# One more visit turns its attention weights on VectorE and DMAs, two visits become a pair, and six steps round two pieces of weights where three did

## The chip, the cores and the metric

The kernel runs on one core of one Trainium2 chip. The metric is device time in microseconds (us) of one execution. The kernel before takes 1389.05 us (median of three). TensorE is PE in the profile, its weight loads PEld, VectorE is DVE, ScalarE is ACT, GpSimd is POOL, SyncE is SP.

## The reference

Threshold attention over 8 batches of 8 heads, 576 positions, head size 64, followed by an MLP with a squared ReLU (condensed here):

```python
scores = scale * np.matmul(q, k.transpose(0, 1, 3, 2))
thresh = np.max(scores, axis=-1, keepdims=True) - tau
scores = np.where(scores >= thresh, scores, -1000000000.0)
attn = np.exp(scores - np.max(scores, axis=-1, keepdims=True))
attn = attn / (np.sum(attn, axis=-1, keepdims=True) + 1e-09)
out = np.matmul(attn, v)                 # (B,H,S,D) -> (B*S, H*D) = (4608, 512)
h = out @ w_in                           # 512 x 2048
r = np.maximum(h, 0.0)
y = (r * r) @ w_out                      # 2048 x 512
```

## The kernel before

Two things run through each other: attention, in *visits* (one pair of heads each) of four or five *steps* (128 query rows each), and the MLP in chunks of 256 tokens, cut into pieces of about 1.76 us of TensorE work that fill the steps.

The attention weights of a step must be transposed before they meet the values. Early visits do it on TensorE (`turn`), later ones on VectorE in blocks of 32x32 (`turn_blocks`), and DMAs then put the blocks in place (`place_blocks`). In the paired form two visits share one step for their last 64 rows each.

```python
def paired(n):
    return n >= 3 * HP            # HP = 4: visit 12 on
def by_dma(n):
    return n >= 3 * HP - 1        # visit 11 goes by DMA, alone
```

Each step stands in the program in this order. The scores need the two score banks of the step before (`s0`, `s1`, one buffer each), so they wait for that step's thresholding:

```python
            if now:
                round_weights(now[0], 0)         # ScalarE prepares the first piece
            if s != 1:
                scores(s)                        # TensorE, then VectorE's maximum
        # ... cut: turn(*old, 0), turn(*old, 1)
        if on:
            exponents(n, i)                      # ScalarE
            for p in now[1:]:
                round_weights(p, 0)              # ScalarE prepares a second piece
            # ... cut
            if lay:
                prep(n + 1)
            elif now:
                for p in now:
                    round_weights(p, 1)          # VectorE: a shift
        # ... cut: mix, fill
        if on:
            threshold(n, i)                      # VectorE: frees the score banks
            # ... cut
            if now:
                round_weights(now[0], 2)         # VectorE: a mask
                round_weights(now[0], 3)         # GpSimd
            for p in now[1:]:
                round_weights(p, 2)
                round_weights(p, 3)
```

`now` holds the pieces of MLP weights that are rounded in this step, none, one or two. There are 32, and their scratch space is the buffer that the turned blocks use later, so that the roundings must be done before the first visit that goes by DMA:

```python
        if s < HP * FIRST:                       # the first eight steps
            x = int(n > 0 and i == 0)
        else:
            x = 2 if (n, i) in ((2 * HP - 2, FIRST + 1), (2 * HP - 1, FIRST + 1), (2 * HP, FIRST)) else 1
        # ... cut
    assert out_from <= first_dma
```

After that, 16 subtractions on VectorE (`some_sums`) make the sums of weights that save an eighth of the later products. Each piece of the first half of MLP chunk 1 brings one along.

## Time and profile before

| kernel before | |
|---|---|
| time, median of 3 | 1389.05 us |
| profiled execution, span | 1389.8 us |
| TensorE busy / idle | 1354.5 / 35.3 us |
| TensorE idle in steps 8 to 29 (53.5 to 191.3 us) | 11.2 us |
| TensorE idle in steps 30 to 44 (to 310.0 us) | 2.7 us |

A step begins here at its first maximum on VectorE. The idle time is the step's length less TensorE's busy time in it. What the table tells is that the kernel is bound by TensorE nearly everywhere, and that what isn't lies in the start and in the steps with roundings. (The 35.3 us also hold 13.7 us before step 8 and 7.6 us after step 44.)

### The profile page before, as it was taken

Reading aid. Unit: us, or ns where it says so; the run is one execution under the profiler, and the core shown is the slowest. Engines: PE = TensorE matmul, PEld = TensorE weight load, DVE = VectorE, ACT = ScalarE, POOL = GpSimd, SP = SyncE. Lnnn points to the kernel's source line nnn. Section 1 sums busy time; section 2 is a strip of 40 time slices with the busy share of each in tenths; the row PEclk is TensorE's granted clock in tenths of the full one; section 3 lists DMA queues with packets and bytes.
Section 4 is the critical chain, followed back from the end, with each engine's and each line's share of the span. In section 5 each row is a group of like instructions: output and inputs, shape, how many; then the busy total and the mean of one; then the engine's idle time right before and its main releaser. Section 6 shows DMA issues by size and latency. Waiting matters only on the chain.

```text
span 1389.8 us, 22678 instructions
## 1 busy us (share of the span) xinstructions
PE 1354.5 (97%) x7576; PEld 1039.6 (75%) x7576; DVE 828.9 (60%) x1866; ACT 439.8 (32%) x1068; POOL 899.3 (65%) x1211
## 2 busy tenths in 40 slices
PE   6898999999999999999999999999999999999998
PEld 5676556777777777787777778777777877788887
DVE  5877675967767676757565757566666665401001
ACT  4776674223232323232223232322222222210110
POOL 3678875668786968686767677676867655422332
PEclk8999999999999999999999999999999999999999
DMA  8763531445545455554445355544445544310000
GB/s 154 157 152 107 143 93 29 88 85 106 115 98 115 97 109 114 105 112 94 92 87 113 76 111 107 112 87 97 93 93 91 118 89 102 64 31 16 0 16 16
DMA packets 407748, 127.95 MB, mean 92 GB/s; under 512 B 390832, under 2 KB 396752, under 8 KB 407632
## 3 DMA queue, kind: packets, MB, share of 16 engines
q1 hardware_dynamic: 385344, 94.57, 36.1%
q0 software_dynamic: 19984, 31.63, 8.4%
q8 instruction: 61, 1.00, 0.3%
q10 hardware_dynamic: 2304, 0.29, 0.2%
q14 instruction: 55, 0.45, 0.1%
HBM read 50.59 MB, written 9.44 MB: 43 GB/s over the span
## 4 chain that ended last, share of the span: by engine, by line
PE 89%; DVE 3%; ACT 3%; POOL 2%; issue 1%; DMA 1%; SPq 0%; DVEq 0%; ACTq 0%; POOLq 0%
PE bank L480 34%; PE bank L552 29%; PE s L246 12%; PE bank L432 11%; PE bank L519 2%; PE bank L330 2%; ACT wT L331 1%; ACT w L284 1%; DVE wo L507 1%; DVE w L296 1%; DVE st L268 1%; POOL g L491 0%; POOL w L306 0%; POOL w_in_sb L147 0%; DVE wo L296 0%
## 5 line engine op out<-in xcount | busy, mean ns | idle before, releaser
L480 PE MATMUL bank<-xT,w_in_sb 128*128 128x256 f32 x2304 | 520.4, 382 | 3.2 <-POOL w_in_sb L147 2.1
L480 PEld LDWEIGHTS bank<-xT,w_in_sb 128*128 128x128 f32 x2304 | 430.8, 190 | 85.8 <-issue 22.2
L268 DVE TENSOR_REDUCE st<-s 128x1 f32<-128x576 f32 x286 | 204.1, 753 | 224.4 <-PE s L246 224.3
L296 DVE SCALAR_TENSOR_TENSOR w<-s,st,w 128x576 f32<-128x576 f32 x269 | 209.2, 815 | 120.6 <-ACT w L284 120.5
L552 PE MATMUL bank<-wo,gsum 128*128 128x256 f32 x1088 | 248.9, 382 | 2.4 <-POOL gsum L470 2.4
L306 POOL TENSOR_SCALAR w<-w,st 128x576 f32<-128x576 f32 x269 | 223.5, 840 | 25.2 <-DVE st L299 19.2
L552 PEld LDWEIGHTS bank<-wo,gsum 128*128 128x128 f32 x1088 | 203.9, 190 | 41.5 <-issue 9.8
L491 POOL TENSOR_TENSOR g<-g 128x512 f32<-128x512 f32 x144 | 152.1, 1057 | 96.4 <-ACT g L490 95.1
L281 ACT ACTIVATE st<-st 128x2 f32<-128x2 f32 (+1 forms) x148 | 30.3, 205 | 566.1 <-DVE st L268 565.4
L552 PE MATMUL bank<-wo,g 128*128 128x256 f32 x816 | 188.3, 382 | 0.0
L284 ACT ACTIVATE w<-s,st 128x576 f32<-128x576 f32 x269 | 183.3, 732 | 0.2 <-ACT st L282 0.2
L370 DVE STREAM_TRANSPOSE turned<-w 128x512 f32<-128x512 f32 (+2 forms) x388 | 168.8, 490 | 18.7 <-DMA wT<-turned 16.7
L246 PE MATMUL s<-kT,qT 64*128 64x288 f32 x1016 | 166.9, 435 | 12.1 <-DVE kT L226 4.9
L304 POOL TENSOR_SCALAR st<-st 128x2 f32<-128x2 f32 (+1 forms) x148 | 32.9, 222 | 221.6 <-DVE w L296 214.4
L552 PEld LDWEIGHTS bank<-wo,g 128*128 128x128 f32 x816 | 153.0, 190 | 30.0 <-issue 8.7
L432 PE MATMUL bank<-wT,vs 128*64 128x128 f32 (+7 forms) x1700 | 167.8, 356 | 5.1 <-ACT wT L331 3.5
L432 PEld LDWEIGHTS bank<-wT,vs 128*64 128x64 f32 (+1 forms) x1700 | 95.5, 136 | 76.8 <-issue 24.6
L490 ACT ACTIVATE g<-bank 128x512 f32<-128x512 f32 x144 | 86.1, 599 | 194.8 <-PE bank L480 194.2
L246 PEld LDWEIGHTS s<-kT,qT 64*128 64x128 f32 x1016 | 94.9, 189 | 69.1 <-issue 49.0
L190 POOL DMA_DIRECT2D vs<-in_v_dram x144 | 90.7, 635 | 0.0
L566 DVE TENSOR_TENSOR gsum<-g 128x512 f32<-128x512 f32 x34 | 23.0, 707 | 110.6 <-PE bank L552 110.6
L145 POOL TENSOR_TENSOR turned<-turned 128x512 f32<-128x512 f32 x32 | 41.1, 1288 | 40.7 <-DVE turned L143 34.9
(80 smaller groups left out, 1006.1 us busy)
## 6 DMA issues: line engine op xcount, KB each, us to landing
wT<-turned SPq DMA_DIRECT2D x800, 72.0 KB, 2.3
out_dram<-osb POOLq DMA_DIRECT2D x34, 256.0 KB, 2.8
wo<-in_moe_w_in_dram SPq DMA_DIRECT2D x16, 512.0 KB, 4.7
wo<-in_moe_w_out_dram SPq DMA_DIRECT2D x16, 512.0 KB, 3.6
ql<-in_q_dram POOLq DMA_DIRECT2D x96, 72.0 KB, 2.7
wT<-turned SPq DMA_DIRECT2D x192, 36.0 KB, 2.3
kl<-in_k_dram POOLq DMA_DIRECT2D x88, 72.0 KB, 3.0
vs<-in_v_dram POOLq DMA_DIRECT2D x48, 128.0 KB, 3.1
```

What stands on the lines that cost most here:

```text
L190: (nc.gpsimd if state["step"] > first_dma + 2 else nc.sync).dma_start(out=to, in_=src)
L246: nc.tensor.matmul(sc[u][to, half, 0:HALF], lhsT, keys[rows, half * HALF:(half + 1) * HALF], start=True, stop=True)
L268: nc.vector.tensor_reduce(out=mx[:, u:u + 1], in_=sc[u][:, :, 0:HALF], axis=AX.XY, op=ALU.max)
L284: nc.scalar.activation(out=w[:, u, :].rearrange("p (h k) -> p h k", h=2), in_=sc[u][:, :, 0:HALF], func=AF.Exp, bias=bias[:, u:u + 1], sca ...
L296: nc.vector.scalar_tensor_tensor(out=wu, in0=sc[u][:, :, 0:HALF], scalar=thr[:, u:u + 1], in1=wu, op0=ALU.is_ge, op1=ALU.mult, accum_out=s ...
L306: nc.gpsimd.tensor_scalar(out=w[:, u, :], in0=w[:, u, :], scalar1=z[:, u:u + 1], scalar2=rcp[:, u:u + 1], op0=ALU.add, op1=ALU.mult)
L370: nc.vector.transpose(wb[:, at:at + k1 - k0, i % 2, :], w[:, u, k0 * 32:k1 * 32].rearrange("p (k q) -> p k q", q=32))
L432: nc.tensor.matmul(ps[u * D:(u + 1) * D, :], vs[n % 2][rows, u * (NBLK + 1) + c, :], wT[rows, NBLK if c == NBLK else u * (NBLK + 1) + c, a ...
L480: nc.tensor.matmul(h[:, x % 2, :], w_in_sb[:, c, f * P:(f + 1) * P], xT[:, c, at:at + TCH], start=(c == 0), stop=(c == NMC - 1))
L490: nc.scalar.activation(out=to, in_=h, func=AF.Relu)
L491: nc.gpsimd.tensor_tensor(out=to, in0=to, in1=to, op=ALU.mult)
L552: nc.tensor.matmul(to, left[:, f, :], wo[:, slot, f, :], start=(f == 0), stop=(f == HF - 1))
```

## The change

The intent: visit 10 is turned on VectorE and DMAs too, visits 10 and 11 become a pair, and the unpaired form goes out of the kernel. So that the roundings are done in time, six steps round two pieces, where three did.

```diff
     def paired(n):
-        return n >= 3 * HP
+        return n >= 3 * HP - 2
     def by_dma(n):
-        return n >= 3 * HP - 1
+        return paired(n)
@@
         else:
-            x = 2 if (n, i) in ((2 * HP - 2, FIRST + 1), (2 * HP - 1, FIRST + 1), (2 * HP, FIRST)) else 1
+            x = 2 if HP <= n < 2 * HP and i == FIRST + 1 or 2 * HP <= n and i == FIRST else 1
@@
-    assert out_from <= first_dma
+    assert out_from <= first_dma + 1
@@ (cut: the unpaired branches of turn_blocks and place_blocks go)
-        if both:
-            odd = M if i in (2, 3) else KB
-            ...
-        else:
-            parts = [(0, 0, KB, 2), (0, M, KB, 0)]
+        odd = M if i in (2, 3) else KB
@@ (cut: when loads, preparations and placings are issued)
-        if not by_dma(n) or i != visits[n][1][0] or paired(n) and n % 2:
+        if i != visits[n][1][0] or not (n % 2 == 0 if paired(n) else paired(n + 1)):
```

## The prediction

> **What bounds the kernel now.** I read the page's shares first, then the slices, the chain that ended last, the groups, and last the window table and timelines of the stretch that the change touches.
>
> ```profile
> PE 1354.5 (97%) x7576; PEld 1039.6 (75%) x7576; DVE 828.9 (60%) x1866; ACT 439.8 (32%) x1068; POOL 899.3 (65%) x1211
> ...
> PE   6898999999999999999999999999999999999998
> ...
> PE 89%; DVE 3%; ACT 3%; POOL 2%; issue 1%; DMA 1%; SPq 0%; DVEq 0%; ACTq 0%; POOLq 0%
> ```
>
> TensorE (PE) is busy for 1354.5 of 1389.8 us and holds 89% of the chain. The other 35.3 us are TensorE idle time. So the result is a sum of two terms: how much TensorE work goes, and how much TensorE idle time comes or goes. Where the idle time lies:
>
> ```profile
> 90.00:230.00 140.00, 129.78 (x961) 86.04 (x959) 98.44 (x214) 92.80 (x229) 106.72 (x116) 1.00 0.42 109
> 230.00:290.00 60.00, 58.93 (x325) 47.22 (x326) 50.76 (x100) 16.68 (x43) 38.21 (x48) 1.00 0.36 65
> 290.00:700.00 410.00, 410.00 (x2222) 310.87 (x2220) 274.99 (x636) 119.14 (x291) 305.60 (x440) 1.00 0.53 105
> ```
>
> (Columns: window, its length, then busy time of PE, weight load, DVE, ACT, POOL.) From 290 us on there is none. It lies in the start, and about 10 us between 90 and 230 us, where roundings of the MLP weights run beside attention. The 60 us after that are the most delicate: TensorE is nearly full, but VectorE (DVE) is at 85%, against 67% later. The rows that the change moves:
>
> ```profile
> L330 PE MATMUL bank<-ident,w 128*128 128x128 f32 x189 | 30.3, 290 | 0.0
> L330 PE MATMUL bank<-ident,wo 128*128 128x128 f32 x63 | 10.6, 298 | 0.0
> L246 PE MATMUL s<-kT,qmid 64*64 64x288 f32 x192 | 15.0, 415 | 0.3 <-DVE qmid L230 0.3
> L246 PE MATMUL s<-kT,qmid 128*128 128x288 f32 x32 | 9.4, 416 | 2.9 <-DVE w L296 1.2 <-ACT wT L343 0.9 <-ACT qmid L221 0.7
> L507 DVE TENSOR_TENSOR wo<-wo 128x512 f32<-128x512 f32 x16 | 15.8, 1023 | 0.0
> ```
>
> A mean in these rows includes pipeline latency; busy time over count is the real cost.
>
> **What the Trainium skill says.** "VectorE: DVE Perf Modes", section "The three transpose paths": VectorE transposes only 32x32 blocks, TensorE a full 128x128 into PSUM. That is why the path taken here needs DMAs to put the blocks in place. The trace agrees in kind (VectorE writes its buffer, 1008 transfers carry it to wT) and shows 0.67 us for a 128x512 block row. "TensorE: Matmul & The Clock Gate", section "Part 3: Packing small matmuls": tiles at different positions of the array run at the same time. The trace agrees: 20 products of a paired visit, 64 rows out each, take 4.72 us, though the groups' own durations add to more. "SBUF — State Buffer", the section on the two sides (list "Reading the diagram"): a VectorE operation with two SBUF inputs and a GpSimd (POOL) operation that reads SBUF hold a shared port pair in turn. The trace agrees: the same subtraction L507 takes 0.68 us in some places and up to 1.85 us in others.
>
> **The change part by part.** A visit is one pair of heads, a step one block of 128 query rows of it. Before, visits 0 to 10 turn weights on TensorE, visit 11 goes by VectorE and DMA but unpaired, visits 12 on go by pairs. After, pairs start at visit 10. I counted both kernels' instructions from the order of the built programs.
>
> TensorE loses, for visit 10 (and the remainders of 10 and 11):
> - 36 full transposes at (30.3 + 10.6) / 252 = 0.162 us: 5.8 us.
> - 10 small ones of the remainder, 0.8 us (the timeline shows a run of 0.47 and one of 0.28).
> - value products in 128-column pieces: four runs of 1.46 and one of 0.95 = 6.8 us, replaced by one wide set of 4.72: 2.0 us.
> - remainder scores: 4 matmuls at 9.4/16 = 0.59 become 8 at 15.0/96 = 0.156 (each matmul has two records): 2.35 - 1.25 = 1.1 us.
>
> Sum 9.7 us, 0.7% of the time. The MLP matmuls are the same in number. ScalarE loses its copies of the turned blocks, which are not on the path.
>
> VectorE gains: per row of blocks two more large transposes and some small ones; from the counts, six at 0.67, two at 0.77, one more 512-wide at 0.67, small ones and a query remainder: 7 us. SP issues 32 + 16 more placing transfers, less 16 of the unpaired kind. GpSimd issues 16 more loads itself at about 0.65 us, 10 us, spread.
>
> Roundings: 32 pieces as before, but done by step 30, not 33. Steps with two pieces go from three to six. The third part of the change is indirect. The single MLP chunk that is ready then has to fill all steps between the end of the roundings and the completion of the next batch: before steps 34 to 43, after steps 31 to 42. Its 30 pieces at 1.76 us are 53 us, so 5.9 us a step before and 4.8 after. The 16 subtractions that prepare the weight sums fall into the same steps.
>
> **Sums by step in that stretch**, from the order after the change and the durations above (subtraction 1.02, large transposes 0.67 or 0.77, reduce 0.75, thresholding 0.86, and so on):
> - steps 31 to 41 after: TensorE 3.5, 9.1, 8.2, 6.4, 6.4, 8.2, 6.4, 7.7, 6.5, 8.2, 6.4, total 76.8; VectorE 5.2, 6.2, 9.2, 9.1, 9.1, 9.2, 6.5, 6.0, 9.7, 6.0, 5.6, total 81.6.
> - steps 35 to 41 before: TensorE 63.0, VectorE 55.4.
>
> VectorE must also wait in each step for the first exponential, 0.5 us where a subtraction is put into the gap and 1.1 where not (the timeline at 243.90 and 271.30 us), some 8 us in 11 steps. So in this stretch after the change VectorE needs near 90 us for what TensorE does in 78 (its sums run 1.5% short of the measured work). TensorE's next scores wait for VectorE's thresholding, since each of the two score banks has one buffer. VectorE may lag 4 us or so without harm, because the work behind the thresholding overlaps, and it makes that up later. New idle time: 90 - 78 - 4 = 8 us. The stretch had 2.1 us of it before; net +6.
>
> The doubled steps: in the two of visits 6 and 7 TensorE idles 1.3 and 1.6 us where single ones have 0.2 to 0.7, and once more 1 us when GpSimd catches up (its row for 105.5 to 114.4 is 8.71 of 8.90). Each costs 1 to 2 us where TensorE has no filler. Three more would be 3 to 5, but the chunk that fills is now compressed too, 3.5 us more TensorE work in steps 8 to 19, and the last one sits where TensorE is full. I take +1.7.
>
> Total: 1389.05 - 9.7 + 6 + 1.7 = 1387.0 us.
>
> **The rivals.**
> (a) TensorE stays the only bound, so that all 9.7 us are won and the early idle shrinks with the filler: 1378 to 1380. For it: the chain is TensorE's and idle is nil after 290 us. Against: VectorE's sums exceed TensorE's in five of the eleven steps, by up to 3 us.
> (b) VectorE becomes the bound for those steps and contention makes it worse: with GpSimd at 7 to 9 us in steps 34 to 36, the subtractions may take 1.4 us, not 1.02; then 12 us or more are lost there and the time is 1390 to 1396. For it: the run of three that took 4.62 us at 247.95 us. Against: much of what the lag costs is absorbed in the PE-heavy steps.
> (c) The placing transfers or the buffer of turned blocks, which the roundings also use, hold VectorE up: 15.5 us of such waits in 28 places later, harmless there because VectorE has slack. In the new stretch it has none; 1 to 3 us.
> (d) The transfers are hidden and roundings ahead of time cost nothing: 1385.
>
> **Range and chances.** The sure part, 9.7 us, caps the gain near 1378; the uncertain part is idle time of 4 to 15 us. I take 1387, range 1380 to 1394. 2% is 28 us, far beyond both, so "within 2%" is nearly certain; a part for an unforeseen stall on the slow side.
>
> **What would show it.** Right: TensorE busy near 1345 us, no L330 matmul after about 195 us, two kinds of rows moving by the counts above, and TensorE idle in a window of about 195 to 285 us of 6 to 10 us, released by VectorE's thresholding (scores of L246 waiting for DVE w), with VectorE above 90% there. Wrong: TensorE above 98% full in that stretch (then a), VectorE's subtractions at 1.4 us (then b), or VectorE waiting there for transfers (then c); or idle time of the middle steps grown by more than 4 us. If TensorE's busy time falls by clearly less than 9 us, my count of the gain is wrong.

## More of the kernel before

The summary of the core has the mean clock that TensorE was granted:

```profile
core 0: 1389.8 us, clock 0.995
```

The waits of VectorE have one row that matters later. Its columns are who waited for whom, us in total, times, and the longest:

```profile
DVE turned L141 <- ACT turned L138: 4.3, 3, 1.6
```

L141 is the shift of a rounding, L138 ScalarE's preparation of it: three waits, in the three steps that round two pieces. And the wait of TensorE's scores for VectorE's thresholding:

```profile
PE s L246 <- DVE w L296: 5.3, 5, 1.8
```

## The result, and the profile after

| | before | after |
|---|---|---|
| time, median | 1388.89 us (4 runs) | 1397.33 us (4 runs) |
| range | 1388.68 to 1389.15 | 1396.48 to 1399.57 |
| profiled execution, span | 1389.8 us | 1394.7 us |
| TensorE busy / idle | 1354.5 / 35.3 us | 1350.8 / 43.9 us |
| idle in steps 8 to 29 | 11.2 us | 14.4 us |
| idle in steps 30 to 44 | 2.7 us | 7.3 us |

The change makes the kernel slower: the ratio is 1.0063, with a 95% interval of 1.0046 to 1.0081. A ratio is the mean time of one kernel's fast runs over that of the other's fast runs of the same rounds, so it isn't quite the ratio of the medians. The profiled execution of after is the fastest of its four runs, and that of before took 1391.53 us, more than any of its four in the table, so the spans show 4.9 us of the 8.4. The interval lies above 1, so the 0.6% is no noise.

The page's shares and its chain, after:

```profile
PE 1350.8 (97%) x7476; PEld 1033.4 (74%) x7476; DVE 840.4 (60%) x1880; ACT 433.0 (31%) x1045; POOL 906.0 (65%) x1226
...
PE 89%; DVE 4%; ACT 3%; POOL 2%; issue 2%; DMA 0%; POOLq 0%; DVEq 0%; SPq 0%; ACTq 0%
```

TensorE still carries the chain. It runs 100 records fewer, but its busy time fell by 3.7 us, not by the 9.7 us that I had counted, and its idle time rose by 8.6 us. The same three windows as in the prediction, after the change (length, busy PE, PEld, DVE, ACT, POOL, granted clock, DMA):

```profile
90.00:230.00 140.00, 128.29 (x908) 85.38 (x907) 102.00 (x213) 85.40 (x209) 104.48 (x114) 0.99 0.42 104
230.00:290.00 60.00, 56.16 (x283) 40.99 (x283) 52.99 (x105) 15.94 (x39) 44.22 (x58) 0.97 0.50 96
290.00:700.00 410.00, 410.00 (x2223) 310.82 (x2220) 276.94 (x640) 118.61 (x292) 306.94 (x444) 1.00 0.54 105
```

Two readings: idle time grew in both of the first windows and stayed nil in the third, and the granted clock, which had been 1.00 in all three, is 0.99 and 0.97. The clock is where most of the missing 6 us of busy time went. In the traces' clock record the granted clock changes only at multiples of 3.41 us; such a stretch is called a slot here, and half clock means a slot that was granted 0.50. Six windows, in pairs, each pair a slot and the one after it:

```profile
61.10:64.50 3.40, 1.19 (x6) 0.96 (x7) 2.86 (x8) 3.16 (x8) 1.04 (x1) 1.00 0.87 206
64.50:67.90 3.40, 3.40 (x27) 2.66 (x24) 3.13 (x6) 1.87 (x5) 2.97 (x4) 0.50 0.90 292
183.90:187.40 3.50, 2.09 (x11) 1.00 (x9) 3.42 (x9) 2.01 (x5) 0.47 (x1) 0.99 0.00 0
187.40:190.80 3.40, 3.40 (x10) 2.35 (x10) 3.40 (x6) 2.29 (x6) 2.87 (x4) 0.50 0.71 110
262.50:265.90 3.40, 1.68 (x8) 1.00 (x8) 2.84 (x9) 2.08 (x5) 1.43 (x2) 1.00 0.02 4
265.90:269.30 3.40, 3.40 (x16) 1.52 (x16) 2.31 (x6) 1.19 (x4) 3.13 (x4) 0.50 0.02 5
```

Each time TensorE is busy for a third to three fifths of a slot, and the next 3.4 us run at clock 0.50. TensorE is busy for all of such a slot, at half the clock. My estimate from these lines: 3.4 x 0.5 = 1.7 us lost in each, 5.1 us in the three. The profile of before has no such slot between its first 30 us and its last 3.

The first eight steps, which the change doesn't touch, took 53.48 us before and 52.01 after: their half clock fell otherwise. The first scores, eight matmul records of one kind, took 2.30 us before (at 8.64 us) and 1.25 after (at 8.50 us). So the busy times are best compared from step 8 on. Here are before, after, and three of the experiments below (`before_late_shift`, `late_shift`, `both_mended`), in this order:

```profile
53.48:1389.76 1336.28, 1314.76 (x7333) 1010.15 (x7332) 793.46 (x1785) 412.60 (x1005) 875.70 (x1169) 1.00 0.44 90
52.01:1394.66 1342.65, 1313.59 (x7233) 1005.97 (x7231) 805.21 (x1799) 405.74 (x982) 882.43 (x1184) 1.00 0.45 91
51.32:1384.47 1333.15, 1314.26 (x7333) 1011.61 (x7332) 796.82 (x1785) 412.34 (x1005) 873.55 (x1169) 1.00 0.44 90
52.23:1386.32 1334.09, 1310.97 (x7233) 1005.16 (x7231) 804.30 (x1799) 405.65 (x982) 882.90 (x1184) 1.00 0.45 92
52.30:1383.13 1330.83, 1307.51 (x7233) 1004.26 (x7231) 802.86 (x1799) 405.29 (x982) 882.92 (x1184) 1.00 0.45 92
```

The last three have half clock in no, two and no slots there, after has three. With the same 7233 matmul records TensorE is busy for 1307.51 us with none, 1310.97 with two and 1313.59 with three: 1.7 to 2.0 us for each slot, a little more than the estimate. And the work that left TensorE, read where no slot of half clock disturbs it, is 1314.26 or 1314.76 less 1307.51: about 7 us, not 9.7.

With that the books close, as far as the profiles go: from step 8 on, about -7 of work, +6 of half clock and +7.5 of idle; before step 8, -1.5 us, which is luck with the clock. That is +5 us, where the spans differ by 4.9.

What TensorE waited for, after:

```profile
PE s L246 <- DVE w L296: 12.5, 11, 2.8
```

Its scores wait for VectorE's thresholding in eleven places, where it was five. And VectorE itself:

```profile
DVE turned L141 <- ACT turned L138: 11.3, 6, 2.5
```

The shift of the second rounding now waits in six steps, for 11.3 us. I had not looked at this row before I predicted.

### The profile page after: what moved, and what is told of

It reads as the page before. It is cut to its first block, busy times and chain, and to the rows that moved or that the text cites. A ratio compares the mean times of both kernels' runs of the same rounds, so it can differ in the third digit from the quotient of the medians.

```text
span 1394.7 us, 22543 instructions
## 1 busy us (share of the span) xinstructions
PE 1350.8 (97%) x7476; PEld 1033.4 (74%) x7476; DVE 840.4 (60%) x1880; ACT 433.0 (31%) x1045; POOL 906.0 (65%) x1226
## 4 chain that ended last, share of the span: by engine, by line
PE 89%; DVE 4%; ACT 3%; POOL 2%; issue 2%; DMA 0%; POOLq 0%; DVEq 0%; SPq 0%; ACTq 0%
PE bank L464 34%; PE bank L536 29%; PE s L246 12%; PE bank L416 10%; PE bank L503 2%; PE bank L330 2%; DVE st L268 1%; ACT w L284 1%; DVE w L296 1%; DVE wo L491 1%; ACT wT L331 1%; POOL w L306 0%; POOL g L475 0%; DVE turned L365 0%; ACT turned L138 0%
## 5 line engine op out<-in xcount | busy, mean ns | idle before, releaser
L536 PEld LDWEIGHTS bank<-wo,gsum 128*128 128x128 f32 x1088 | 203.9, 190 | 41.2 <-issue 10.2
L365 DVE STREAM_TRANSPOSE turned<-w 128x512 f32<-128x512 f32 (+2 forms) x403 | 175.4, 490 | 15.2 <-DMA wT<-turned 13.6
L416 PE MATMUL bank<-wT,vs 128*64 128x320 f32 (+7 forms) x1640 | 168.8, 367 | 4.6 <-ACT wT L331 3.4
L190 POOL DMA_DIRECT2D vs<-in_v_dram x156 | 98.1, 634 | 0.0
```

Source lines behind the costliest of these rows:

```text
L190: (nc.gpsimd if state["step"] > first_dma + 2 else nc.sync).dma_start(out=to, in_=src)
L365: nc.vector.transpose(wb[:, at:at + k1 - k0, i % 2, :], w[:, u, k0 * 32:k1 * 32].rearrange("p (k q) -> p k q", q=32))
L416: nc.tensor.matmul(ps[u * D:(u + 1) * D, :], vs[n % 2][rows, u * (NBLK + 1) + c, :], wT[rows, NBLK if c == NBLK else u * (NBLK + 1) + c, a ...
L536: nc.tensor.matmul(to, left[:, f, :], wo[:, slot, f, :], start=(f == 0), stop=(f == HF - 1))
```

## The experiments

All experiments gave a correct result except the one that is marked. The kernel before was run beside each; its median was 1389.76 us beside the first four and 1390.1 to 1390.3 beside the others, which ran on another chip. So compare ratios.

| run | median us | ratio to before | 95% interval | clock of the runs |
|---|---|---|---|---|
| after | 1397.33 | 1.0063 | 1.0046 to 1.0081 | 0.988 to 0.992 |
| roundings_alone | 1407.07 | 1.0116 | 1.0098 to 1.0135 | 0.987 to 0.991 |
| pairs_alone (wrong result) | 1400.83 | 1.0077 | 1.0064 to 1.0090 | 0.990 to 0.991 |
| late_shift | 1389.28 | 1.0001 | 0.9989 to 1.0013 | 0.989 to 0.993 |
| sums_spread | 1395.81 | 1.0036 | 1.0023 to 1.0049 | 0.990 to 0.992 |
| kept_busy | 1398.33 | 1.0054 | 1.0041 to 1.0066 | 0.993 to 0.994 |
| kept_busy_three | 1396.30 | 1.0039 | 1.0026 to 1.0052 | 0.992 to 0.994 |
| before_late_shift | 1387.25 | 0.9980 | 0.9968 to 0.9993 | 0.994 to 0.995 |
| both_mended | 1384.95 | 0.9964 | 0.9951 to 0.9976 | 0.992 to 0.996 |
| early_both | 1382.14 | 0.9946 | 0.9932 to 0.9959 | 0.993 to 0.995 |
| before_early_both | 1393.24 | 1.0023 | 1.0009 to 1.0037 | 0.990 to 0.994 |
| early_later | 1382.47 | 0.9943 | 0.9929 to 0.9957 | 0.993 to 0.994 |
| early_later_sums | 1382.60 | 0.9951 | 0.9937 to 0.9965 | 0.992 to 0.994 |

My theory after the first look: the doubled steps cost idle time because something in them holds up VectorE's thresholding; the stretch where VectorE transposes and subtracts costs the rest; and idle time is paid twice, since half clock may follow. The rivals: the roundings cost nothing and the loss sits in the stretch; GpSimd's backlog is what costs; transfers hold VectorE up.

**roundings_alone: the doubled roundings in the kernel before.** Visit 10 stays on TensorE.

```diff
-            x = 2 if (n, i) in ((2 * HP - 2, FIRST + 1), (2 * HP - 1, FIRST + 1), (2 * HP, FIRST)) else 1
+            x = 2 if HP <= n < 2 * HP and i == FIRST + 1 or 2 * HP <= n and i == FIRST else 1
```

> The kernel before with one part of the change: six steps with two roundings, not three; visit 10 still turned on TensorE. My theory (each doubled step makes VectorE's thresholding wait, TensorE idles 1 to 2.5 us there and in some executions the next 3.4 us run at half clock): about 1395 us, 5 to 7 above before, with TensorE idle up 3 us in steps 8 to 29 and half-clock stretches after 60 us. Rival (the loss sits in the stretch where VectorE does transposes and subtractions together): as before, 1388 to 1390. Rival (the filler compressed into fewer steps covers the doubling): 1388 to 1389.

Measured: 1407.07 us, 1.2% above before, worse than the whole change. The direction is that of my theory, the size is more than I expected. Its profiled execution was the fastest, 1401.52 us. In it TensorE idles 2.8 us more than before in steps 8 to 29, as expected. The rest came from a place that I hadn't thought of: 7.7 us of idle time in steps 30 to 44 (2.7 before), since the roundings' earlier end also thins out the filler of those steps. And three slots ran at half clock, at 61.7, 123.1 and 287.0 us. The longest single wait there, and VectorE's shifts, in two views:

```profile
PE s L246 <- DVE qT L226: 4.0, 1, 4.0
```

```profile
DVE turned L141 <- ACT turned L138: 12.1, 6, 2.5
```

The first is the scores of step 41 waiting for the next visit's queries, which VectorE lays out behind the thresholding of step 40; the slot at 287.0 us follows it. One subtraction of 1.0 us stands ahead in that step, and TensorE has only 9 MLP matmul records there, where before has 25; which of the two carries the wait was not separated. The six executions also differ by 8.7 us, and the slower ones have the lower clock: 1401.52 us at 0.991, 1405.6 to 1410.2 at 0.987. That fits slots of half clock that come in some executions and not in others; it was not varied on its own here, and of the slower ones there is no profile. So the roundings cost something, but this run mixes their own cost with that of the shifted filler. The next two runs separate them.

**pairs_alone: the change without the doubling.** The roundings then run until step 33, beside the first transposes of visit 10.

```diff
-            x = 2 if HP <= n < 2 * HP and i == FIRST + 1 or 2 * HP <= n and i == FIRST else 1
+            x = 2 if (n, i) in ((2 * HP - 2, FIRST + 1), (2 * HP - 1, FIRST + 1), (2 * HP, FIRST)) else 1
@@
-    assert out_from <= first_dma + 1
```

> The changed kernel with only three doubled steps, so that rounding runs on until step 33, beside the first transposes of visit 10. My theory: the 9.7 us of TensorE work go, the middle steps are as in before, but steps 31 to 34 have too little TensorE work to cover VectorE, 8 us or more of idle time there and some half-clock stretches: 1390 to 1398. Rival (the doubling is all of the loss): 1380 to 1384.

Measured: 1400.83 us, just above my range, and a wrong result (relative error 0.57). I had not foreseen the wrong result, though the assertion that I took away stands for it: rounding scratch and turned blocks share a buffer. The time is still of use. Steps 8 to 29 are as in before (11.1 us idle), and steps 30 to 44 idle 14.2 us, of which one wait of 7 us:

```profile
PE s L246 <- DVE qT L226: 7.0, 1, 7.0
```

Behind it the clock was half for four slots (213.0 to 226.7 us).

So the rival that the doubling is all of the loss is out: without it the pairs have too little TensorE work around them, and they need the roundings to be over by then.

**late_shift: the second piece's shift moved behind the thresholding.** This is the experiment that decides on the doubled steps. In the program of the changed kernel VectorE has the shift of the second piece ahead of the thresholding, and it needs ScalarE's preparation, which stands behind both exponentials.

```diff
             elif now:
-                for p in now:
-                    round_weights(p, 1)
+                round_weights(now[0], 1)
@@
             for p in now[1:]:
                 assert not lay
+                round_weights(p, 1)
                 round_weights(p, 2)
```

> The changed kernel with one thing moved: of a step's second rounding, the first VectorE operation (the shift) stands behind the thresholding and not ahead of it, so that the thresholding no longer waits for ScalarE's preparation of that piece. My theory: idle time of the doubled steps falls by 3 to 4 us and the half-clock stretches near 64 and 187 us go, 3.4 us more: 1389 to 1392. Rival (GpSimd's backlog of roundings is what costs): no change, 1396 to 1398.

Measured: 1389.28 us, ratio 1.0001: the move takes back 8 us. VectorE in step 9 of the changed kernel (start, length, what, and in brackets the idle time before it and what ended it):

```profile
58.68 0.42 DVE L141 TENSOR_SCALAR turned<-turned 128x512 uint32<-128x512 uint32 x1
61.57 0.86 DVE L141 TENSOR_SCALAR turned<-turned 128x512 uint32<-128x512 uint32 x1 [2.47 <-ACT turned L138]
62.35 0.81 DVE L296 SCALAR_TENSOR_TENSOR w<-s,st,w 128x576 f32<-128x576 f32 x1
```

and in the same step with the late shift:

```profile
58.90 0.42 DVE L141 TENSOR_SCALAR turned<-turned 128x512 uint32<-128x512 uint32 x1
60.53 0.82 DVE L296 SCALAR_TENSOR_TENSOR w<-s,st,w 128x576 f32<-128x576 f32 x1 [1.21 <-ACT w L284]
```

The thresholding starts 3.0 us after the maximum began (57.49) and not 5.1 (57.27). The row of six waits on L138 is gone from VectorE's waits. TensorE's idle time falls from 14.4 to 8.4 us in steps 8 to 29, and the half-clock slot near 187 us goes. The one near 63 us stays: step 9 still idles 1.8 us. So does the one behind step 37, now at 257.9 us. GpSimd's work is the same in both, so its backlog was not what cost the 8 us.

**before_late_shift: the same move in the kernel before**, as a control, which has three doubled steps.

> The kernel before with the same one move as in the run with the late shift. It has three doubled steps, none of them followed by half clock. Theory: it gains 0.8 to 1.3 us of idle time in each, 1386 to 1388, far less than the 8 us that the move gave to the changed kernel. Rival (the move helps for another reason, in all steps): 1380 to 1384.

Measured: 1387.25 us, ratio 0.9980, as expected. The move pays where two pieces are rounded in a step. It gives 0.2% here and 0.6% in the changed kernel, which has twice as many such steps, and where half clock followed some of them.

**sums_spread: the 16 subtractions over more steps.**

```diff
-        if j == PLAIN:
+        if j == PLAIN and x % 2:
             posts.append(lambda: some_sums(1))
```

> The changed kernel with the 16 preparing subtractions spread over steps 33 to 40, at one for every second piece of the MLP chunk, where they stood in 32 to 37. My theory (VectorE bounds steps 33 to 37): idle time there falls from 7 to about 4 us and the half-clock stretch near 266 us goes: 1392 to 1394. Rival (what VectorE waits for there is the placing transfers or GpSimd): no change, 1396 to 1398.

Measured: 1395.81 us, above the expected range. The direction is right and the size is less than expected. The half-clock slot near 266 us is gone, but the profile has another at 124.2 us, behind step 18, so there are still three, as in after. Idle time in steps 30 to 44 is also still 6.5 us, against 7.3: part of it moved to steps 38 to 40, where the remaining subtractions now stand, and part was never VectorE's. Steps 30 to 32 have 3.4 us of idle in both, since step 31 has no MLP piece at all: the last weights are not yet usable. The window from 260 to 290 us of this run shows VectorE as the full engine:

```profile
260.00:290.00 30.00, 26.92 (x148) 17.81 (x147) 27.88 (x60) 5.88 (x16) 18.07 (x26) 1.00 0.50 91
```

**kept_busy and kept_busy_three: matmuls that nobody needs, where TensorE idled.** These test the clock. The first adds 50 matmuls of the identity in seven places, the second 24 in the three places that half clock had followed (the second's edit, shortened):

```diff
+        for x in range({10: 8, 28: 5, 38: 11}.get(s, 0)):
+            idle = ...          # a bank that is read no more
+            nc.tensor.matmul(bank[idle][:, 0:P], ident, ident, start=True, stop=True)
         if i == NBLK and paired(vis):
```

> The changed kernel with 50 extra matmuls of the identity (128 columns, about 0.22 us each, 11 us of work in all) put ahead of the scores at the seven places where TensorE idled over 1 us. Their results are never read. Theory (part of the loss is half clock, which follows slots of low TensorE activity): the half-clock slots near 64, 187 and 266 us go, and the time falls by 2 to 5 us although work is added: 1392 to 1395. Rival (the granted clock has nothing to do with activity, or the idle time alone is the loss): 1397 to 1401.

> The changed kernel with 24 extra matmuls, 6 us of work, only at the three places that half-clock slots followed in its profile (ahead of the scores of steps 10, 28 and 38), the first into a bank that nobody reads at that time: the last try filled step 9 late and made it longer. Theory: the half-clock slots near 64, 187 and 266 us go, 5 us, and some of the added work spills: 1392 to 1395, faster than the changed kernel by 2 us or more. Rival: 1397 or more.

Measured: 1398.33 and 1396.30 us. Both miss the time that I expected. The clock does what the theory says, in two of three places in the first run (near 63 us a slot with TensorE busy for 1.30 of 3.40 us was still followed by half clock) and in all three in the second:

```profile
60.40:63.80 3.40, 3.40 (x39) 3.01 (x37) 0.92 (x2) 3.39 (x10) 3.17 (x4) 1.00 0.92 212
63.80:67.20 3.40, 2.27 (x16) 1.66 (x16) 3.33 (x11) 2.81 (x8) 0.92 (x1) 1.00 0.82 259
186.10:189.60 3.50, 3.18 (x35) 2.28 (x29) 2.58 (x6) 2.96 (x7) 1.64 (x2) 1.00 0.00 0
189.60:193.00 3.40, 3.40 (x17) 2.00 (x16) 3.35 (x8) 1.17 (x5) 1.87 (x2) 1.00 0.31 51
265.20:268.60 3.40, 3.06 (x20) 2.14 (x19) 2.83 (x9) 2.03 (x5) 1.47 (x2) 1.00 0.03 6
268.60:272.00 3.40, 3.40 (x29) 1.96 (x30) 2.31 (x6) 1.24 (x4) 3.13 (x4) 1.00 0.00 0
```

All at clock 1.00, and the mean clocks of its six executions are 0.992 to 0.994, where those of the changed kernel are 0.988 to 0.992. In exchange a new half-clock slot came at 74.0 us, behind a slot that idled 2.0 us. That half clock follows low activity is thus shown. What a slot costs in device time these two runs don't show: the added work spilled over, and the second run's ratio of 1.0039 lies below 1.0063 but the intervals overlap. In busy time it is the 1.7 to 2.0 us above.

All fourteen profiles together tell more. From 31 us on, up to 15 us from the end, half clock followed 18 slots that had run at full clock: all eleven in which TensorE was busy for 1.40 us or less of the 3.41, seven of the 26 between 1.49 and 2.04, and none of the thousands above. So where a gap falls in its slots decides too: step 18 idles 2.0 us before its scores in after, in roundings_alone and in sums_spread alike. In the latter two this left 1.38 us of work in one slot, and half clock followed; in after the slot kept 1.85 us, and it didn't.

**both_mended and early_both: do the mends add, and can the change be made to pay?** The first has late_shift and sums_spread together. The second has only three doubled steps in addition, and rounds the three pieces that this leaves over in the first 50 us:

```diff
-            x = int(n > 0 and i == 0)
+            x = int(n > 0)
         else:
-            x = 2 if HP <= n < 2 * HP and i == FIRST + 1 or 2 * HP <= n and i == FIRST else 1
+            x = 2 if (n, i) in ((2 * HP - 2, FIRST + 1), (2 * HP - 1, FIRST + 1), (2 * HP, FIRST)) else 1
```

> The changed kernel with the late shift and with the subtractions spread. Theory (the two losses are separate): the gains add, 8 and 1.5 us: 1387 to 1389. If spreading removes half clock near 258 us that the late shift alone still had: 1386.

> As the one before, but with only three doubled steps: the three pieces that this leaves over are rounded in the second steps of visits 1 to 3, in the first 50 us. Theory: the doubled step of visit 4, which still left 1.8 us of idle and a half-clock slot near 63 us with the late shift, goes: 1383 to 1387, the fastest. Against: the first steps are bound by the chain of scores, maximum, exponential and thresholding, and a piece more may lengthen each by 1 us: then 1386 to 1390.

Measured: 1384.95 and 1382.14 us. Both are faster than the ranges that I expected, though the kernel before was also some 0.5 us slower on this chip. By the ratios both mends together give 0.99%, and singly 0.62% and 0.27%: a sum, within the intervals. The third gave another 2.8 us; the two intervals still overlap a little. The profile of early_both has no half clock after the start, and idle times of 7.2 us in steps 8 to 29 and 5.7 in steps 30 to 44:

```profile
90.00:230.00 140.00, 132.84 (x928) 90.74 (x927) 103.70 (x222) 84.52 (x207) 105.67 (x119) 1.00 0.45 107
230.00:290.00 60.00, 57.75 (x317) 41.06 (x316) 53.44 (x114) 15.32 (x42) 47.29 (x67) 1.00 0.51 99
```

The clock is 1.00 again in both windows. TensorE's total busy time is 1343.6 us, 10.9 below before, but 2.7 of that lie in the first eight steps, where before ran longer at half clock. From step 8 on it is 1306.59 us, some 8 us below the kernel before, with two matmul records more ahead of step 8. That is near the 7 us above and not the 9.7.

**before_early_both: the three mends in the kernel before.**

> The kernel before (visit 10 turned on TensorE) with all three mends of the fastest so far: late shift, spread subtractions, early roundings. It tells what the pairs alone are worth where the roundings cost the same. Theory: 9.7 us of work against 3 us of new idle time in the stretch, so the version with pairs (1382) is 5 to 7 us faster: this one 1387 to 1389. Rival (the mends are all of the gain and the pairs give nothing): 1382 to 1384.

Measured: 1393.24 us, slower than before itself, so the expectation failed. It was meant as the fair partner of early_both, and it isn't one. Spreading the subtractions put three of them, 2.3 us together, ahead of step 40's maximum and so of the next visit's queries, for which TensorE then waited 5.2 us:

```profile
PE s L246 <- DVE qT L226: 5.2, 1, 5.2
```

Half clock followed for two slots, and for two more at 199.7 us, behind steps 31 and 32. Step 40 also has only 4 MLP matmul records here, where early_both has 22, and roundings_alone had a like wait with one subtraction; so that the subtractions carry it is likely and not shown. The 11 us between this and early_both are therefore not the worth of the pairs; they contain this wait and these slots.

**early_later and early_later_sums: more filler for steps 30 to 32.** The first spreads the first MLP chunk over three more steps (`out_from += 3`), the second also does two of the subtractions already in step 32.

> The fastest so far with the first MLP chunk spread over three more steps (to step 33), so that steps 30 to 32, which had 3.4 us of TensorE idle for want of filler, get some of it. Theory: that idle time halves: 1379 to 1382. Against: the subtractions then fall again into four steps, and the middle steps lose filler: 1382 to 1385.

> The version with the first chunk spread to step 33, and in addition two of the 16 subtractions done already in step 32, behind pieces of that chunk's second half. Theory: step 40, where TensorE waited 3 us for VectorE with three subtractions in it, keeps one of them, and its idle time falls by half, with the half-clock slot behind it: 1379 to 1381, the fastest. Rival (the wait at step 40 has another cause): 1382 to 1383 as without them.

Measured: 1382.47 and 1382.60 us, the same as early_both. In the first, steps 30 to 32 lose most of their idle time, but step 33 idles 1.9 us and step 40 3.0 us with half clock behind it, and steps 8 to 29, whose filler was taken, idle 10.2 us where it was 7.2. In the second, that wait is gone (idle in steps 30 to 44 falls to 3.8 us), but step 33, with a single MLP piece, idles 2.9 us and two half-clock slots follow. The second expectation failed in its time and held in its mechanism: one wait was exchanged for another.

## Why the prediction was wrong

The prediction was 1387 us with a range of 1380 to 1394. It was 1397.33. Point by point, by its own steps:

- *"TensorE loses ... Sum 9.7 us."* "TensorE busy near 1345 us" was measured as 1350.8, and this step failed twice. **The sum had no term for the granted clock.** It took TensorE's time per matmul as fixed, though I quoted a page of the skill that treats the clock gate, and a profile whose first 30 us show half clock. In its place: three slots of half clock, about 6 us of busy time, each behind a slot in which TensorE idled 1.4 to 2.2 us. And the work itself was taken too high: about 7 us left TensorE. "Busy time over count is the real cost" is the slip: a group's busy time holds a tail that the next matmul covers. In the timeline of before three transposes take 0.38 us up to the next matmul's start (90.49 to 90.87 us), 0.13 each where I took 0.162, which makes some 1.2 us of the 36 (my estimate). The remainder scores, by their rows in before_late_shift and both_mended (9.5 to 7.2 us and 15.0 to 16.7), gave 0.6 us, not 1.1. The rest of the difference is not traced.
- *"The doubled steps ... I take +1.7."* This is the term that was mis-sized, and its reason was wrong. Idle time in steps 8 to 29 rose by 3.2 us, and two of the half-clock slots followed such steps (9 and 27), 3.4 us by the estimate: 6.6 in place of 1.7. I had put it down to missing filler and to GpSimd catching up. late_shift shows that VectorE's second shift, waiting ahead of the thresholding for ScalarE, carried it: one move gave 8 us back. The view that told of it was there before: three waits, 4.3 us.
- *"New idle time: 8 us ... net +6."* Nearly right: 7.3 us in steps 30 to 44, net +4.6. VectorE did bind in steps 34 to 37, and the scores did wait for the thresholding. But about 3.4 us of that idle time lie in steps 30 to 32, where VectorE isn't the bound but TensorE lacks an MLP piece; I hadn't separated that. The half-clock slot after step 37 was again not in the sum. (In the prediction's own lists VectorE's sums exceed TensorE's in seven of the eleven steps, not five, and steps 34 to 43 and 31 to 42 are ten and twelve, where its shares of 5.9 and 4.8 us take nine and eleven. The total doesn't rest on either.)
- *Rival (b)*, subtractions of 1.4 us in steps 34 to 36: it came half true. All sixteen took 1.10 on average, against the 1.02 that I used, but the ten in steps 34 to 36 took 1.31. The loss of 12 us or more that it forecast didn't come: 7.3 us in steps 30 to 44, of which steps 34 to 37 have 3.8. *Rival (c)*, transfers that hold VectorE up: in the stretch the view of waits has two, 1.7 us together, at 289 and 297 us, where TensorE didn't idle; VectorE's waits for transfers were 13.6 us in all, less than before. It is out.
- *"no L330 matmul after about 195 us", "VectorE above 90% there"*: the last L330 matmul started at 205.7 us, since the steps before it took longer. VectorE was at 53.0 of 60 us in the window from 230 to 290 us, 88%, and 95% between 231 and 260.
- The chances (within 2%) held, because the whole change is worth well under 2%: no merit of the reasoning.

What stays open: what decides between 1.49 and 2.04 us of activity in a slot. A slot with TensorE busy for 1.85 of 3.40 us (122.5 to 125.9 us in the profile after) was not followed by half clock, one with 2.09 of 3.50 was. And the worth of the pairs alone, with roundings of equal cost, was not isolated, since before_early_both brought a wait of its own.

## What to carry to other kernels

In a kernel that one engine binds, price the idle gaps of that engine twice: the gap, and what the granted clock does behind it; gaps of 1.4 to 2.8 us, and the slots behind three of them, cost more here than the work that the change removed. Price removed matmuls by the time to the next matmul's start, not by a group's busy time. When a change repeats a pattern more often (two roundings in a step), look in the old profile for the wait which that pattern already has, because it is multiplied too. And where an operation frees a buffer that the bounding engine waits for, nothing should stand ahead of it in its engine's order that waits for a third engine: moving one such operation turned a loss of 0.6% into none, and with two more mends into a gain of 0.5%.

## What the Trainium skill lacked or had wrong

- "TensorE: Matmul & The Clock Gate", section "HAM oscillation — how this bites in real kernels", gives the rule as no idle gaps of TensorE over about 3.4 us. Here half clock followed gaps of 1.4 to 2.8 us: a slot with TensorE busy for 2.09 of 3.50 us was enough (183.9 us after the change). The length of a slot, 3.41 us, and the clock of one half agree with that page's Part 1.
- The same page doesn't say which share of a slot must be busy. In these fourteen profiles half clock followed every slot with 1.40 us or less of 3.41 (eleven), seven of 26 between 1.49 and 2.04, and none above; what decides in between stays open.
- "SBUF — State Buffer", list "Reading the diagram": it describes the shared port as a lock, without a figure for instructions of a case like this. The 128x512 subtraction took 0.65 us at best and 1.54 us at worst after the change, 1.10 on average; all seven of 1.47 us and more overlapped a GpSimd TENSOR_TENSOR (on `g` or `gsum`).
